# Attention tokens held as 64 rows of 7 chunks, with q and k on alternating partitions

## The chip, the cores and the metric

The kernel runs on one core of a Trainium2 chip. The metric is the device time of one execution in microseconds, as the median of several runs. Beside those runs there is one execution that was recorded by the hardware profiler; all durations of single instructions come from it.

## What is computed

Attention with normalised queries and keys over 8 batches of 12 heads, 448 tokens and 64 features, followed by a token mixer of rank 32 and a two-layer MLP over 768 features with 3072 hidden units:

```python
q_n, k_n = rmsnorm(q, g_q), rmsnorm(k, g_k)             # over the 64 features
attn = softmax(q_n @ k_n.T / 8)                         # 448 x 448, for 96 heads
x = heads_beside_each_other(attn @ v)                   # 8 x 448 x 768
u = x + (x.transpose(0, 2, 1) @ U @ V).transpose(0, 2, 1)   # U 448 x 32, V 32 x 448
out = u + relu(u @ w_ch1) @ w_ch2                       # w_ch1 768 x 3072, w_ch2 3072 x 768
```

## The kernel before

**Layout.** Two neighbouring heads form a pair `p` (48 pairs, 6 to a batch); two pairs form a load group `t` (24 groups). The 448 tokens of a head lie as 112 partitions of 4 tokens each: token 4p + j is row p of chunk j. So q, k and v of a head are loaded as 112 rows of 1024 B (`heads`, `load`, `load_v`; 128 rows are read where there is something behind, and 16 of them are not used). The products are worked on in the chunk order: column c of the queries is row c % 112 of chunk c // 112, and the results for 128 such columns at a time are one tile of x (`OFFS` gives the start of each of the four; odd batches are shifted by 64 columns, so that a tile can hold the end of one batch and the start of the next).

**One pair.** `squares` squares q and k (on GpSimd, a few on ScalarE), `reduce` sums over the features on VectorE into `rs_bank`, `rsqrt` takes the power of -1/2 on ScalarE as Ln and Exp, `scale` multiplies on VectorE and casts to bf16 (`qkn`). The normalised rows are turned so that the features lie on the partitions. Pairs 0 to 11 turn on TensorE (`turn`: 8 transposes into one PSUM bank), and `take_q` and `take_k` copy the result to `qkT`, the first with the gain `gg` = g_q * g_k; pairs 12 to 47 turn by a transposing DMA (`dma_transposes`), and `gains` multiplies on ScalarE in place. Then `scores` makes for each of the 4 chunks of keys a 112 x 448 block for each of the two heads (8 matmuls; their stationary operand is 128 columns of `qkT`, of which 16 belong to what lies behind the chunk, except for pair 0, which takes 112), `expo` takes the exponential of both heads' blocks in one ScalarE instruction (4 to a pair), `products` multiplies E with the values and a column of ones (16 matmuls for each head), and `normalize` divides by the sum (3 VectorE instructions for each head). `cast_v` makes the bf16 values of a group on GpSimd.

**The mixer and the MLP.** `mix_to` forms U's product (`Ub` holds U's rows in the order of the x tiles), `mix_x` and `mix_u` add V's product to x. `mlp` runs 24 groups of 6 matmuls into `hT` (`ph`, then a Relu on ScalarE or VectorE), and then 24 matmuls for each half tile of the output (`po`), adds x and stores the rows by chunks (`store`).

**U.** U comes in the same 112-row layout (`Uf`, `Us`). `setup_U` moves its rows on TensorE with shifted identities (14 matmuls, the word `pU` of the head), and one ScalarE copy (`Ub:a`) brings them to `Ub`. The cast of V's columns into chunk order and two copies to `Vsh` are in `setup_late` (the word `late`), on GpSimd.

**Order.** The scheduler is off (`tc.manual_schedule()`): each engine runs its instructions in the order in which the program issues them. The first batch's attention is written out as the list `HEAD`: `sq` squares, `R` reduce, `q` rsqrt, `S` scale (`Sq` on VectorE and `Sk` on GpSimd for pair 0), `T` transposes (the digit behind a colon is the PSUM bank, a letter the engine: `a` ScalarE, `v` VectorE, `p` GpSimd), `Eq` and `Ek` the copies of q and k, `SC` one chunk's scores, `X` its exponential, `V` the products and `N` the normalisation of one head, `MT`, `t`, `MU`, `u` the mixer of the first batch, `B` the first MLP matmuls that were put ahead, `F` matmuls without use that keep TensorE busy, `w` the loads of weights (GpSimd's queue), `cast` the values' cast, `ld` the loads of U and V, `G` the gain column. After a word named in `ISSUE`, further loads are issued on SyncE's queue. From there on `weave` spreads the next batch's `attention` and `mixing` over the matmuls of the running batch's `mlp`; at the end of the head `mlp(0)` begins with its fifth group.

## Time and profile before

| | |
|---|---|
| median of 5 runs | 600.79 us (600.41 to 603.1) |
| the profiled execution | 602.41 us, of which 600.5 us are the span of its instructions |
| TensorE matmuls busy | 582.7 us, 97% of the span |
| weight loads of TensorE (beside the matmuls) | 319.1 us |
| VectorE, ScalarE, GpSimd busy | 296.1, 264.7, 127.3 us |
| transfers | 72.27 MB, mean 120 GB/s |
| granted TensorE clock, mean | 0.994 |

In the views below, a group of instructions is named by its line, its engine and output<-input. A timeline row gives the start in us, the duration, the instruction, and in brackets how long its engine stood idle ahead of it and which instruction or transfer ended that. A row by stretches gives for each engine its busy us and its instructions, then the granted clock, the share of the DMA engines and GB/s.

### The profile page before, as it was taken

To read this page: it belongs to the slowest core of one execution; us is meant where nothing else is said; L and a number is where in the kernel's file an instruction comes from. 1 tells how busy PE (TensorE), PEld (TensorE's weight loads), DVE (VectorE), ACT (ScalarE), POOL (GpSimd) and SP (SyncE) were. 2 spreads that over 40 slices of the span, in tenths; PEclk is the share of its full clock that TensorE was granted. 3 is DMA by queue.
4 is the path that set the end of the run, shared out by engine and by line. 5 is a ranking of instruction groups with operands and counts; after the bars stand their busy time and mean duration, and the time that the engine had idled before them with its cause. 6 is when DMAs were issued, how large, how long until landed. Compare 5 with 4: busy or idle time off the path is not lost.

```text
span 600.5 us, 11297 instructions
## 1 busy us (share of the span) xinstructions
PE 582.7 (97%) x4723; PEld 319.1 (53%) x4723; DVE 296.1 (49%) x604; ACT 264.7 (44%) x425; POOL 127.3 (21%) x113
## 2 busy tenths in 40 slices
PE   6799998999999999999999999999999999999996
PEld 3465555444565555544565556544465555554563
DVE  4785878345453566454453665545454462521111
ACT  5867551466503772076620875056640476112200
POOL 6793230333030330220330131303303000000000
PEclk9889999999999999999999999999999999999999
DMA  8999995854353544544264652833544210140011
GB/s 269 271 232 238 237 238 82 213 136 121 63 151 83 138 137 126 127 135 70 87 171 67 154 136 51 201 83 97 136 121 106 63 28 6 45 89 0 1 53 52
DMA packets 107799, 72.27 MB, mean 120 GB/s; under 512 B 56616, under 2 KB 104104, under 8 KB 107748
## 3 DMA queue, kind: packets, MB, share of 16 engines
q1 hardware_dynamic: 96292, 61.56, 40.5%
q0 software_dynamic: 11168, 9.73, 9.9%
q8 instruction: 37, 0.61, 0.4%
q10 hardware_dynamic: 288, 0.26, 0.1%
q14 instruction: 14, 0.11, 0.1%
HBM read 56.78 MB, written 11.01 MB: 113 GB/s over the span
## 4 chain that ended last, share of the span: by engine, by line
PE 82%; DVE 2%; ACT 1%; issue 0%; DVEq 0%; ACTq 0%
PE po L406 35%; PE ph L386 33%; PE o L289 6%; PE sc L276 6%; PE px L356 1%; DVE rs_bank L212 1%; PE pm L331 1%; DVE osb L410 1%; ACT E L281 0%; DVE qkn L229 0%; PE px L353 0%; ACT hT L389 0%; PE px L354 0%; DVE x L301 0%; DVE xs L304 0%
## 5 line engine op out<-in xcount | busy, mean ns | idle before, releaser
L281 ACT ACTIVATE E<-sc 112x896 bf16<-112x896 f32 x192 | 172.9, 914 | 176.9 <-PE sc L276 176.8
L406 PE MATMUL po<-w2b,hT 128*128 128x384 bf16 x1344 | 237.7, 326 | 2.2 <-DVE osb L410 1.3
L406 PEld LDWEIGHTS <-hT 128*128 128x128 bf16 x1344 | 126.4, 98 | 90.5 <-issue 11.5
L386 PEld LDWEIGHTS <-w1b 128*128 128x128 bf16 x1128 | 102.7, 98 | 105.6 <-issue 19.7
L209 POOL TENSOR_TENSOR sq<-qk 112x1024 f32<-112x1024 f32 x42 | 79.3, 1896 | 316.3 <-DMA qk<-in_k_dram 247.6
L386 PE MATMUL ph<-uB,w1b 128*128 128x512 bf16 x576 | 132.6, 379 | 0.0
L389 ACT ACTIVATE hT<-ph 128x512 bf16<-128x512 f32 (+1 forms) x122 | 66.8, 547 | 107.1 <-PE ph L386 106.6
L386 PE MATMUL ph<-uA,w1b 128*128 128x384 bf16 x552 | 100.5, 326 | 0.4 <-DVE x L358 0.3
L391 DVE TENSOR_SCALAR hT<-ph 128x384 bf16<-128x384 f32 (+1 forms) x66 | 41.1, 622 | 93.4 <-PE ph L386 93.2
L289 PEld LDWEIGHTS <-E 112*128 112x128 bf16 x1536 | 61.8, 99 | 19.2 <-issue 5.0
L410 DVE TENSOR_TENSOR osb<-po,x 128x384 f32<-128x384 f32 x48 | 26.8, 558 | 73.5 <-PE po L406 73.2
L212 DVE TENSOR_REDUCE rs_bank<-sq 112x16 f32<-112x1024 f32 (+1 forms) x45 | 54.0, 1199 | 8.8 <-ACT sq L207 6.2
L289 PE MATMUL o<-va,E 112*128 112x65 bf16 x1344 | 56.9, 194 | 0.5 <-DVE xs L304 0.5
L276 PE MATMUL sc<-qkT 64*128 64x448 bf16 x376 | 55.2, 359 | 1.4 <-ACT E L281 0.8
L229 DVE TENSOR_TENSOR qkn<-qk,rs_bank 112x1024 bf16<-112x1024 f32 (+1 forms) x46 | 55.2, 1202 | 2.6 <-ACT rs_bank L221 2.4
L300 DVE RECIPROCAL rec<-o 128x4 f32<-128x4 f32 x84 | 15.2, 181 | 70.5 <-PE o L289 70.2
L276 PEld LDWEIGHTS <-qkT 64*128 64x128 bf16 (+1 forms) x384 | 13.4, 95 | 34.8 <-issue 29.4
L358 DVE TENSOR_TENSOR x<-px,x 128x384 bf16<-128x384 f32 x48 | 25.9, 553 | 11.9 <-PE px L356 11.9
L301 DVE TENSOR_TENSOR x<-o,rec 128x192 bf16<-128x192 f32 x84 | 30.0, 357 | 2.9
L195 POOL CAST va<-vt 112x1024 bf16<-112x1024 f32 x23 | 23.9, 1042 | 1.3 <-PE sc L276 1.3
L267 ACT ACTIVATE qkT<-qkT,gg 128x448 bf16<-128x448 bf16 x36 | 23.8, 662 | 0.0
L304 DVE TENSOR_TENSOR xs<-o,rec 64x64 bf16<-64x64 f32 x84 | 18.3, 218 | 0.7
(83 smaller groups left out, 183.2 us busy)
## 6 DMA issues: line engine op xcount, KB each, us to landing
qk<-in_q_dram SPq DMA_DIRECT2D x44, 256.0 KB, 4.7
qk<-in_k_dram SPq DMA_DIRECT2D x44, 256.0 KB, 5.0
vt<-in_v_dram SPq DMA_DIRECT2D x22, 512.0 KB, 5.7
w1b<-in_moe_w_ch_dram POOLq DMA_DIRECT2D x6, 768.0 KB, 18.1
w2b<-in_moe_w_ch_dram POOLq DMA_DIRECT2D x6, 768.0 KB, 38.5
out_dram<-osb SPq DMA_DIRECT2D x8, 336.0 KB, 2.8
out_dram<-osb SPq DMA_DIRECT2D x8, 288.0 KB, 2.9
out_dram<-osb SPq DMA_DIRECT2D x8, 240.0 KB, 2.8
```

The lines of the kernel that those rows point to most:

```text
L209: nc.gpsimd.tensor_tensor(dst, src, src, OP.mult)
L212: nc.vector.tensor_reduce(rs_of(p).rearrange("p (s h j) -> p s h j", s=2, h=2)[:, :, hs], sqs[p].rearrange("p (s h j d) -> p s h j d", s=2 ...
L229: eng.tensor_tensor(qkns[p][:, :, c].rearrange("p j g d -> p g j d"), qk_of[t][0:SP, a].rearrange("p s h (j d) -> p (s h) j d", d=D)[:, c] ...
L276: nc.tensor.matmul(sc[0:n, hh, 0:S], flat[pp, c:c + n], blocks(p)[pp, :, 0], start=True, stop=True)
L281: nc.scalar.activation(Es[p % NE][:, :, PAD + kc * S:PAD + (kc + 1) * S], scs.pop((p, kc))[0:SP, :, 0:S], AF.Exp, scale=float(D) ** 0.5)
L289: nc.tensor.matmul(o[:, i, :], E[:, hh, c:c + P], va[:, hl, kc, :], start=(kc == 0), stop=(kc == NJ - 1))
L301: nc.vector.tensor_tensor(x3[:, :, d0:d0 + D], o[:, t0:t0 + 3, 0:D], rec[:, t0:t0 + 3].rearrange("p c -> p c ()").to_broadcast([P, 3, D]), ...
L386: nc.tensor.matmul(ph, w1b[:, dc, hc * P:(hc + 1) * P], u[:, dc, :], start=(dc == 0), stop=(dc == KD - 1))
L389: nc.scalar.activation(hT[:, hc, 0:n], ph, AF.Relu)
L391: nc.vector.tensor_relu(hT[:, hc, 0:n], ph)
L406: nc.tensor.matmul(po, hT[:, hc, i * P:(i + 1) * P], w2b[:, half, hc], start=(hc == 0), stop=(hc == KH - 1))
L410: nc.vector.tensor_add(osb[:, hs], po, xt[i][:, hs])
```

## The change

Tokens lie as 64 rows of 7 chunks: token 7p + c is row p of chunk c. q's rows go to the even and k's rows to the odd partitions of one 128-partition tile (`qk_of[t][s::2]`), so each squares, reduce and transpose handles q and k together; `load` issues 2 transfers to a group in place of 4, `load_v` 3 in place of 1. `scale` is two instructions, for chunks 0 to 3 and 4 to 6, that write to alternating places of `qkn`, so that the chunk order becomes 0, 4, 1, 5, 2, 6, 3 and two chunks make 128 columns. A pair is turned in 7 transposes of 128 x 128. In the result every second column is a query and every second a key: `take_q` and `gains` read every second column into a tile of their own (`qT`), `take_k` copies the others to the odd columns of `qkT`, and `scores` reads its 128 stationary columns from every second column of `qkT`. The 448 keys are three blocks of 128 and one of 64; the last block's other 64 rows are zero in k, get an exponent of -30000 (`none`), and meet values of chunk 3 loaded a second time. U is loaded twice, to both halves of the partitions, and GpSimd casts it in 4 pieces to `Ub`; V's cast is 3 pieces. `setup_U` and the words `pU` and `Ub:a` are gone. The list `HEAD` is written anew; in place of `Sq`, `Sk`, `Tq`, `Tk` pair 0 has `Se` (chunks 0 to 3, VectorE), `So` (chunks 4 to 6, GpSimd) and one `T`.

```diff
-    NJ = 4
-    SP = S // NJ
+    NC = 7
+    SP = S // NC
...
-    SQK = 2 * NJ * SP
+    NK = 4
...
+    CHUNKS = (0, 4, 1, 5, 2, 6, 3)
...
-    Uf = consts.tile([SP, NJ * rank], FP32, name="Uf")
-    Us = consts.tile([SP, NJ, rank], BF16, name="Us")
+    Uf = consts.tile([P, NC, rank], FP32, name="Uf")
...
-    Es = [consts.tile([SP, 2, PAD + NJ * S + PAD], BF16, name=f"E{i}") for i in range(NE)]
+    Es = [consts.tile([P, 2, PAD + NK * S + PAD], BF16, name=f"E{i}") for i in range(NE)]
-    qkTs = [consts.tile([P, SQK + 16], BF16, name=f"qkT{i}") for i in range(NQ)]
-    qkL = [consts.tile([P, 2, 2, 2, NJ * D], FP32, name=f"qk{i}") for i in range(2)]
-    vL = [consts.tile([P, HG, NJ * D], FP32, name=f"vt{i}") for i in range(2)]
+    qTs = [consts.tile([P, S], BF16, name=f"qT{i}") for i in range(NQ)]
+    qkTs = [consts.tile([P, 2 * NK * P], BF16, name=f"qkT{i}") for i in range(NQ)]
+    qkL = [consts.tile([P, 2, 2, NC * D], FP32, name=f"qk{i}") for i in range(2)]
+    vL = [consts.tile([P, HG, NK * D], FP32, name=f"vt{i}") for i in range(2)]
...
+        nc.gpsimd.memset(none[0:SP], 0.0)
+        nc.gpsimd.memset(none[SP:], -30000.0)
...
     def setup_late():
-        nc.gpsimd.tensor_copy(Us, Uf.rearrange("p (j r) -> p j r", j=NJ))
-        nc.gpsimd.tensor_copy(V4.rearrange("r (j p) -> r j p", j=NJ), Vf.rearrange("r (p j) -> r j p", j=NJ))
+        for par in range(2):
+            for half in range(2):
+                i0, n, c0 = ((0, 4, 0), (0, 3, 4), (1, 3, 4), (0, 4, 0))[2 * par + half]
+                rows = slice(half * SP, (half + 1) * SP)
+                nc.gpsimd.tensor_copy(Ub[rows, par, i0:i0 + n], Uf[rows, c0:c0 + n])
+        Vc = Vf.rearrange("r (p c) -> r c p", c=NC)
+        for half in range(2):
+            at = V4[:, 0:S - SP].rearrange("r (i n p) -> r n i p", n=2, p=SP)[:, half]
+            nc.gpsimd.tensor_copy(at, Vc[:, 4 * half:4 * half + 3])
+        nc.gpsimd.tensor_copy(V4[:, S - SP:], Vc[:, 3])
...
         if part == "U":
-            nc.gpsimd.dma_start(Uf, moe_U.rearrange("(p j) r -> p (j r)", j=NJ))
+            nc.gpsimd.dma_start(Uf.rearrange("p c r -> p (c r)"),
+                                bass.AP(moe_U.tensor, moe_U.offset, [[0, 2], [NC * rank, SP], [1, NC * rank]]))
...
-    def setup_U(pU):
...
     def heads(x, h, n):
-        rows = P if h + n < B * H else SP
-        src = x.rearrange("b h s d -> (b h) s d")[h:h + n].rearrange("h (p j) d -> p h (j d)", j=NJ)
-        (ps, _), (hs, _), (ls, ln) = src.ap
-        return rows, bass.AP(src.tensor, src.offset, [[ps, rows], [hs, n], [ls, ln]])
+        return x.rearrange("b h s d -> (b h) s d")[h:h + n].rearrange("h (p c) d -> p h (c d)", c=NC)
     def load_pair(eng, t, s, a, hs=slice(0, 2)):
-        rows, src = heads((q, k)[s], HG * t + 2 * a + hs.start, hs.stop - hs.start)
-        eng.dma_start(qk_of[t][0:rows, a, s, hs], src)
+        h = HG * t + 2 * a
+        eng.dma_start(qk_of[t][s::2, a, hs], heads((q, k)[s], h + hs.start, hs.stop - hs.start))
     def load(t):
-        for a in range(2):
-            for s in range(2):
-                load_pair(nc.sync, t, s, a)
+        for s in range(2):
+            nc.sync.dma_start(qk_of[t][s::2].rearrange("p a h c -> p (a h) c"),
+                              heads((q, k)[s], HG * t, HG))
     def load_v(t):
-        rows, src = heads(v, HG * t, HG)
-        nc.sync.dma_start(v_of[t][0:rows], src)
+        src = heads(v, HG * t, HG)
+        for rows, c0, c1, at in ((0, 0, 4, 0), (SP, 4, 7, 0), (SP, 3, 4, 3)):
+            nc.sync.dma_start(v_of[t][rows:rows + SP, :, at * D:(at + c1 - c0) * D], src[:, :, c0 * D:c1 * D])
...
-            nc.scalar.activation(copy, rs[:, 8:16], AF.Exp, scale=-0.5)
+            nc.scalar.activation(copy, rs, AF.Exp, scale=-0.5)
...
-    def scale(p, eng=nc.vector, c=slice(0, 4), rs=None):
+    def scale(p, parts=(0, 1), eng=nc.vector, rs=None):
         t, a = divmod(p, 2)
         if p not in qkns:
-            qkns[p] = norm.tile([SP, NJ, 4, D], BF16, tag="qkn", name="qkn", bufs=3)
-        n = c.stop - c.start
-        rs = rs_of(p)[:, c.start * NJ:c.stop * NJ] if rs is None else rs
-        eng.tensor_tensor(
-            qkns[p][:, :, c].rearrange("p j g d -> p g j d"),
-            qk_of[t][0:SP, a].rearrange("p s h (j d) -> p (s h) j d", d=D)[:, c],
-            rs.rearrange("p (g j) -> p g j ()", j=NJ).to_broadcast([SP, n, NJ, D]),
-            OP.mult)
...
-    def turn(p, s, pt):
-        for j in range(NJ):
-            nc.tensor.transpose(pt[:, s, j], qkns[p][:, j, 2 * s:2 * s + 2].rearrange("p h d -> p (h d)"),
-                                ident[:SP, :SP])
+            qkns[p] = norm.tile([P, NC, 2, D], BF16, tag="qkn", name="qkn", bufs=3)
+        rs = (rs_of(p) if rs is None else rs).rearrange("p (h c) -> p h c ()", h=2)
+        for part in parts:
+            c = slice(0, 4) if part == 0 else slice(4, NC)
+            n = c.stop - c.start
+            eng.tensor_tensor(
+                qkns[p][:, part::2].rearrange("p c h d -> p h c d"),
+                qk_of[t][:, a].rearrange("p h (c d) -> p h c d", d=D)[:, :, c],
+                rs[:, :, c].to_broadcast([P, 2, n, D]),
+                OP.mult)
+    def turn(p, pt):
+        for c in range(NC):
+            nc.tensor.transpose(pt[:, c], qkns[p][:, c].rearrange("p h d -> p (h d)"), ident)
+        del qkns[p]
     def take_q(p, pt):
-        nc.vector.tensor_scalar(blocks(p)[:, :, 0], pt[:, 0], gg, None, OP.mult)
+        nc.vector.tensor_scalar(qTs[p % NQ], pt.rearrange("p c r -> p (c r)")[:, 0::2], gg, None, OP.mult)
     def take_k(p, pt, copy=nc.vector.tensor_copy):
-        copy(k_side(p)[:, 0:SQK].rearrange("p (j s r) -> p j s r", j=NJ, s=2)[:, :, 1], pt[:, 1])
+        copy(qkTs[p % NQ][:, 1:2 * S:2], pt.rearrange("p c r -> p (c r)")[:, 1::2])
...
     def dma_transposes(p):
-        nc.sync.dma_start_transpose(out=qkTs[p % NQ][:, 0:SQK].rearrange("p (m r) -> p m r", r=SP),
-                                    in_=qkns.pop(p).rearrange("p j g d -> p (j g d)"))
+        nc.sync.dma_start_transpose(out=qkTs[p % NQ][:, 0:2 * S].rearrange("p (c r) -> p c r", r=P),
+                                    in_=qkns.pop(p).rearrange("p c h d -> p (c h d)"))
     def gains(p):
-        qT = blocks(p)[:, :, 0]
-        nc.scalar.activation(qT, qT, AF.Copy, scale=gg)
+        nc.scalar.activation(qTs[p % NQ], qkTs[p % NQ][:, 0:2 * S:2], AF.Copy, scale=gg)
     def scores(p, kcs):
-        flat, n = k_side(p), SP if p == 0 else P
         for kc in kcs:
             sc = ps_s.tile([P, 2, 512], FP32, tag="s", name="sc")
-            c = (2 * kc + 1) * SP
             for hh in range(2):
                 pp = slice(hh * D, (hh + 1) * D)
-                nc.tensor.matmul(sc[0:n, hh, 0:S], flat[pp, c:c + n], blocks(p)[pp, :, 0],
+                nc.tensor.matmul(sc[:, hh, 0:S], qkTs[p % NQ][pp, 2 * kc * P + 1:2 * (kc + 1) * P:2], qTs[p % NQ][pp],
                                  start=True, stop=True)
             scs[p, kc] = sc
     def expo(p, kc):
-        nc.scalar.activation(Es[p % NE][:, :, PAD + kc * S:PAD + (kc + 1) * S], scs.pop((p, kc))[0:SP, :, 0:S],
-                             AF.Exp, scale=float(D) ** 0.5)
+        nc.scalar.activation(Es[p % NE][:, :, PAD + kc * S:PAD + (kc + 1) * S], scs.pop((p, kc))[:, :, 0:S],
+                             AF.Exp, scale=float(D) ** 0.5, **({"bias": none} if kc == NK - 1 else {}))
...
     def store(b, c0, c1, osb, r0):
-        orow = out[b].rearrange("(p j) d -> j p d", j=NJ)
-        for j, p0, p1, r in segments(c0, c1):
-            nc.sync.dma_start(orow[j, p0:p1, :], osb[r0 + r:r0 + r + p1 - p0, :])
+        orow = out[b].rearrange("(p c) d -> c p d", c=NC)
+        for n in range((c1 - c0) // SP):
+            r = r0 + n * SP
+            nc.sync.dma_start(orow[CHUNKS[c0 // SP + n]], osb[r:r + SP, :])
...
     HEAD = """
-        sq00:a R00 sq01:a R01 q0 gg Sk0 sq1:a G Sq0 Tq0:0 Tk0:1 F8:2 R1 ld:U ld:V sq2:a Eq0 q1 sq3:p
-        Ek0:a S1 SC00 X00 SC01 R2 T1:0 cast0 X01 Eq1 SC02 F1:1 q2 SC03 F3:1 Ek1:v X02 S2 SC10 T2:0
-        sq4:p X03 SC11 X10 R3 Eq2 V00:1 q3 SC12 Ek2:v X11 w10 S3 V01:0 SC13 late X12 R4 T3:2 X13
-        SC20 Eq3 SC21 Ek3:a V11:2 sq5:p X20 N00 V10:1 N01 N10 q4 X21 SC22 S4 pU:0 w11 X22 SC23
-        SC30 Ub:a MT0:0 w12 R5 X23 t0:a T4:1 cast1 SC31 Eq4 X30 V20:0 N11 w13 q5 w14 SC32 Ek4:a S5
-        V21:2 cast2 X31 MT1:1 t1:v SC33 X32 N21 T5:1 Ek5:v X33 SC40 w15 Eq5 MU1:2 w20 SC41 u1:v
-        X40 V31:1 X41 N20 w21 SC42 V30:2 N31 X42 sq6:p SC43 N30 X43 MU0:0 SC50 u0:v MT3:1 t3:v
-        MT2:2 SC51 sq7:p X50 V40:0 R6 X51 SC52 X52 V41:1 N40 SC53 R7 B00 t2:a X53 MU2:0 B01 u2:v
-        V50:2 N50 q6 B10 V51:0 N41 B02 MU3:2 N51 u3:a B11 MT4:1 t4:v B12 MT5:0 S7 MU4:1 t5:a B03
-        MU5:0 u4:a S6 B13 B04 u5:a B14 B05 B15
+        sq00:a R00 sq01:a R01 q0 gg So0 sq1:a G Se0 R1 T0:0 F4:1 Ek0:a ld:U q1 ld:V Eq0 S1 SC00
+        sq2:a sq3:p X00 SC01 F1:0 R2 X01 T1:0 cast0 q2 SC02 F1:1 Ek1:v X02 Eq1 SC03 F3:0 S2
+        sq4:p SC10 X03 T2:0 R3 X10 Eq2 SC11 F1:1 SC12 w10 q3 Ek2:v X11 R4 late V00:1 V01:0 X12
+        S3 SC13 SC20 X13 N01 T3:2 q4 SC21 Eq3 X20 V11:0 X21 sq5:p Ek3:v SC22 S4 V10:2 N11 w11
+        X22 N10 SC23 X23 SC30 w12 T4:0 X30 R5 cast1 MT1:2 SC31 X31 t1:v SC32 V21:2 Eq4 q5 w13
+        Ek4:v SC33 N00 MT0:0 w14 X32 V20:1 S5 t0:a SC40 X33 cast2 N20 T5:0 Eq5 SC41 X40 w15
+        V31:1 SC42 w20 Ek5:v X41 N21 MU1:0 N31 w21 X42 MT2:2 SC43 X43 u1:v V30:1 sq6:p N30 SC50
+        t2:a MU0:0 X50 SC51 u0:v X51 V41:1 N41 SC52 sq7:p MT3:0 X52 V40:2 R6 t3:a SC53 X53 MU2:1
+        u2:a MU3:0 N40 B00 u3:a V50:2 R7 B01 N50 MT4:0 t4:a V51:1 N51 q6 B02 B10 B03 B11 S7
+        MT5:0 t5:a MU4:1 u4:v B12 MU5:0 u5:v B13 B04 B14 S6 B05 B15
     """
```

## The prediction

> **What bounds the kernel now.** I read the page's busy shares first.
>
> ```profile
> PE 582.7 (97%) x4723; PEld 319.1 (53%) x4723; DVE 296.1 (49%) x604; ACT 264.7 (44%) x425; POOL 127.3 (21%) x113
> ```
>
> TensorE holds the kernel on average, but the change touches mostly the other engines. So I asked for the stretches: the start, the head's two halves with the slow part between them, the first MLP, and the rest.
>
> ```profile
> 0.00:12.50 12.50, 8.19 (x35) 3.44 (x37) 4.92 (x7) 6.06 (x12) 7.68 (x29) 1.00 0.81 257
> 12.50:25.70 13.20, 10.85 (x146) 6.67 (x145) 11.26 (x21) 12.07 (x22) 9.05 (x10) 1.00 1.12 284
> 25.70:34.20 8.50, 6.48 (x74) 4.12 (x72) 5.22 (x16) 5.59 (x9) 8.50 (x10) 0.60 1.18 252
> 34.20:45.75 11.55, 11.27 (x156) 7.30 (x153) 9.98 (x27) 7.69 (x15) 9.76 (x8) 1.00 1.21 229
> 45.75:105.00 59.25, 56.83 (x541) 32.78 (x539) 44.91 (x92) 28.58 (x47) 15.18 (x10) 1.00 1.04 198
> 105.00:600.50 495.50, 489.09 (x3783) 264.78 (x3780) 219.81 (x444) 204.71 (x323) 77.13 (x49) 1.00 0.40 98
> ```
>
> From 105 us on TensorE is busy for 489.1 of 495.5 us, 4.6 of the rest being the end. There only fewer or shorter TensorE instructions help. Before 45.75 us the head is a chain over all engines. Its worst stretch is 25.70 to 34.20, where GpSimd is busy all the time and the granted clock is 0.60. GpSimd's timeline says why.
>
> ```profile
> 8.56 0.70 POOL L609 TENSOR_TENSOR grow<-grow 1x64 f32<-1x64 f32 x2 [3.95 <-DMA grow<-in_g_k_dram]
> 9.22 1.03 POOL L229 TENSOR_TENSOR qkn<-qk,rk 112x512 bf16<-112x512 f32 x1
> 10.21 0.75 POOL L147 DMA_DIRECT2D Uf<-in_moe_U_dram  x1
> 10.95 0.73 POOL L149 DMA_DIRECT2D Vf<-in_moe_V_dram  x1
> ...
> 21.65 1.00 POOL L131 CAST V<-Vf 128x448 bf16<-128x448 f32 x1 [4.09 <-DMA Vf<-in_moe_V_dram]
> ...
> 23.10 1.89 POOL L209 TENSOR_TENSOR w2b<-hT 112x1024 f32<-112x1024 f32 x1
> 24.95 1.72 POOL L166 DMA_DIRECT2D w1b<-in_moe_w_ch_dram  x2
> 26.64 1.06 POOL L195 CAST va<-vt 112x1024 bf16<-112x1024 f32 x1
> ```
>
> The gains land at 8.56, hence the late scale of pair 0 and the late issue of U and V; V lands at 21.65, and behind its cast stand a square, two weight issues and the values' cast of group 1. TensorE stands before that cast:
>
> ```profile
> 27.76 1.04 PE L289 MATMUL bank<-va,E 112*128 112x65 bf16 x16 [2.02 <-POOL va L195]
> ```
>
> After this gap 16 products take 1.04 us instead of 0.68, until about 34.2.
>
> **The change part by part.**
>
> *Start.* Ahead of the gains in the queues stand 1024 KB of q and k (four transfers of 128 KB, two of 256), landed by 7.96 (issue at 2.16 plus 5.8 to landing); now 896 KB. An eighth of some 6 us is 0.75; I take 0.7, ends 0 and 1.0. GpSimd's scale of pair 0 has 384 elements: from its rows on GpSimd, 1.03 us for 512 and 1.89 for a square of 1024, 0.82 us, so 0.2 less. So U's load starts 0.85 us sooner, at about 9.35. The seven transposes end at about 9.85. Pair 0's copy of k no longer stands behind `q1`, which held it to 11.10; behind it now stands a square of 0.95 us (0.63 for 512 elements, 1.06 for 1024). First exponential: 9.85 + 0.55 + 0.95 = 11.35, now 12.78. This 1.4 us reaches the end only as far as the next wait moves too.
>
> *U and V on GpSimd.* V: 10.1 + its 10.7 us to landing = 20.8. U landed in 6.3 us when read once; now it is read twice by one transfer, as V is read four times. Ends: 6.3, and 13.4, the longest of the q and k loads then; I take 10.7, as V's is the only repeated load: 20.05. Four casts at 0.30 (the row of Us) end at 21.25. V's 448 elements in three pieces cost 1.00 plus two starts, 1.25 in all, the two copies 0.45: 22.95 against 23.10. The square shrinks by an eighth to 1.66; with 1.72 and 1.0 the values' cast ends at 27.3, against 27.7: gain 0.4. With U at 6.3 us it is 0.85; with 13.4 it is a loss of 2.3. [...]
>
> *What stands behind that cast.* Today the waiting products (`V20`) are queued ahead of `SC32`, so ScalarE runs dry after `X31`. The new list has `SC32` ahead of `V21`: one exponential more (0.85 us) is done in the gap. Gain 0.85. The gap itself stays about 2 to 2.5 us, so the slow clock may come again. If it does, the stretch behind it holds as much TensorE work as before and gives some 0.2 back: 0.4 + 0.85 - 0.2, 1.05 us in all. If it does not, the four gaps of ScalarE before its exponentials from 28 to 33.65 us (1.27, 0.79, 0.46, 0.32) shrink to that of the wait: some 1.8 more, 2.85. The trace has one such gap, and the clock slowed after it; how near it was to not slowing no row tells, so I take the middle, 1.95.
>
> *No TensorE for U.* 14 matmuls (0.5 us) and a ScalarE copy (0.39) leave, at 23 us, ahead of the gap: they lengthen it by what they save. Nothing.
>
> *VectorE.* Reduces have 896 elements for 1024: 1.22 becomes 1.09 (from 0.70 for 512). The two scales, 0.69 (the row for 512) and 0.56, less overlap, against 1.21: nothing. The copies from PSUM read every second bf16 column: today 0.45 and 0.38; upper end the f32 cast of 384 elements, 0.558, plus 64 more, 0.63 and 0.69. So per pair of the first twelve -0.13 to +0.35 us; I take +0.35, the row that reads a 4-byte step. In the head the wait above hides it. From 45.75 to 85 us VectorE is busy three quarters of the time: +0.1. From 85.8 to 96.8 the chain that ended last runs over VectorE with three reduces and two scales and no copies: -0.4, of which TensorE, which waits there 1.7 us in four pieces, gets half. Together -0.1.
>
> *Scores.* Same 384 matmuls, same 448 columns, same 192 exponentials of 896. New is the stationary operand with a step of two columns, of which the trace has no example. The nearest rows are contiguous:
>
> ```profile
> L276 PEld LDWEIGHTS <-qkT 64*128 64x128 bf16 x376 | 12.8, 94 | 33.8 <-issue 28.4 <-ACT rs_bank L221 1.6 <-ACT E L281 1.3
> ...
> L276 PEld LDWEIGHTS <-qkT 64*112 64x112 bf16 x8 | 0.7, 124 | 1.1 <-issue 0.9
> ```
>
> The load of 112 columns takes longer than that of 128. Bounds: 0, and these 30 ns for each load if a step costs the same; no gain, as the number of columns stays. I take 0, since the operand has 128 columns as the faster row. [...]
>
> *At nothing.* DMA transposes: 36 of 112 x 1024 become 128 x 896, the same bytes, 1.22 us each on SyncE, two pairs ahead; uncovered, 36 times any excess, on a queue that idles most of the time. `load_v` adds two issues of 0.4 us to a group, `load` drops two of 0.45. `gains` (0.66) on ScalarE, under half busy after 105 us. Stores keep two transfers to a tile. The weights land ahead of their use by 5 us at least (issue at 36.5 plus 39.0, used at 80.6), so 2 us less head still fits, the more with fewer bytes of q and k.
>
> *Sum:* -1.95 - 0.1, about -2.0 us. The profiled execution's 602.41 (span 600.5 and 1.9 around it) would become 600.4; it stood 1.6 above the median, so I apply the difference to the median 600.79: 598.8, from 599.6 (slow clock again) to 597.9 (not). A measurement here tells 0.3% from no change, 1.8 us.
>
> **The rivals.**
>
> *A, slower: the stepped weight load.* Outside the head stand 336 of the 384 loads, on the engine without slack. Pair 0's four matmuls with loads of 112 took 0.58 us, those with 128 columns 0.55: 7.5 ns each, 2.5 us in all; with the full 30 ns, 10.1. That gives 601.3 to 608.9, say 605. It decides from 6 ns a load (2.0 / 336) and is slower by 0.3% from 11. For it: both loads of a chunk stand ahead of two matmuls that run side by side, and two of these pairs take 0.49 us where 448 columns each go through. Against it: the unchanged number of columns.
>
> *B, U lands late.* At 13.4 us to landing the cast loses 2.3, the exponential ahead of it gives 0.85: 2.3 - 0.85 + 0.2 - 0.1 = +1.55 with the slow clock, -0.25 without: 602.3 to 600.5, say 601.5. For it: U lands first in GpSimd's order, so V's cast stands behind it. Against it: V's row.
>
> *C, the gap closes.* If V lands 2 us sooner, because the queues hold fewer and longer pieces, TensorE does not wait and the clock stays: a further 2.0 us on the lower end, 595.9. Against it: U's casts alone would hold GpSimd until 21.25.
>
> **How the numbers follow.** The forecast has 0.62, of which 0.38 beyond 1.8 us and 0.24 within; A 0.20 (0.18 slower, 0.02 within); B 0.10 (0.07 within, 0.03 slower); C 0.08 (faster). So faster 0.46, same 0.33, slower 0.21. The range 596.4 to 606.0 leaves out C and the upper two fifths of A, 0.16 together; the forecast's own is 597.5 to 600.2.
>
> **What would show it.** The first exponential at about 11.4 us; U landing by 20; the values' cast ending at 27.3; `mlp(0)` starting about 43.8 instead of 45.75; the stretch after it as long as now. Weight loads of the scores above 100 ns, or pairs of their matmuls longer than 0.36 us after 105 us, would prove A. U's casts starting after 21.5 would prove B. A copy from PSUM near 0.4 us would void VectorE's surplus.

## The result: 604.60 us against 601.09, slower by 0.5%

The changed kernel took 604.60 us in the median of 24 runs (600.95 to 607.36), the kernel before 601.09 us beside it (45 runs, 599.76 to 604.96). The ratio is 1.0054 (1.0041 to 1.0067). On a second chip it was 1.0030 (1.0006 to 1.0054). The prediction said 598.8; its range reached up to 606.0 for rival A, which is not what happened. That 604.60 lies inside that range is luck: the forecast was a gain, and the part of the range above 602.3 was there for a cost that did not arise.

The profiled execution of the changed kernel took 603.29 us (span 601.5). It lies 1.3 below its median, while that of the kernel before (602.41) lies 1.3 above its own. So the two profiles show 1.0 us (in their spans) of a loss of 3.5; the rest of it has to be looked for in what varies between executions.

The stretches of the changed kernel, as the prediction showed them for the kernel before: busy us and instructions of PE, PEld, DVE, ACT, POOL, then granted clock, share of the DMA engines, GB/s.

```profile
0.00:12.50 12.50, 9.02 (x42) 3.85 (x42) 5.88 (x9) 6.95 (x14) 9.28 (x32) 1.00 0.78 218
12.50:25.70 13.20, 8.07 (x85) 4.54 (x83) 8.86 (x16) 8.53 (x15) 7.27 (x13) 0.80 1.13 219
25.70:34.20 8.50, 7.67 (x108) 4.88 (x107) 8.14 (x25) 7.55 (x12) 8.50 (x10) 0.90 1.17 263
34.20:45.75 11.55, 11.40 (x154) 7.48 (x153) 10.03 (x29) 7.35 (x15) 8.91 (x8) 1.00 1.20 225
45.75:105.00 59.25, 55.74 (x527) 31.91 (x526) 45.60 (x97) 28.90 (x47) 15.19 (x12) 1.00 1.06 200
105.00:600.50 495.50, 490.16 (x3789) 265.38 (x3787) 214.00 (x480) 207.70 (x323) 69.83 (x49) 1.00 0.41 95
```

Two rows tell of a loss. From 12.5 to 25.7 us TensorE is busy for 8.07 us (10.85 before), the slow clock has moved here, and the DMA engines move 219 GB/s in place of 284 at the same busy share. From 45.75 to 105 us TensorE idles 1.1 us more. GpSimd's timeline shows what stands first:

```profile
6.52 0.70 POOL L582 TENSOR_TENSOR grow<-grow 1x64 f32<-1x64 f32 x2 [1.13 <-DMA grow<-in_g_k_dram]
7.96 1.01 POOL L149 DMA_DIRECT2D Uf<-in_moe_U_dram  x1
8.96 0.72 POOL L152 DMA_DIRECT2D Vf<-in_moe_V_dram  x1
...
19.18 1.68 POOL L200 TENSOR_TENSOR w2b<-hT 128x896 f32<-128x896 f32 x1 [5.03 <-DMA hT<-in_k_dram]
...
26.36 1.74 POOL L159 DMA_DIRECT2D w1b<-in_moe_w_ch_dram  x2
28.08 1.06 POOL L185 CAST va<-vt 128x1024 bf16<-128x1024 f32 x1
```

The gains land early, as forecast. Then the square of pair 4 (`sq4`; the expectations call it the fourth pair's) waits 5.0 us for the keys of group 2 (`load(2)`): issued at 8.36 us, landed at 19.2. Before the change pair 4's keys were there in time, and the square ran without a wait:

```profile
14.54 1.89 POOL L209 TENSOR_TENSOR w2b<-hT 112x1024 f32<-112x1024 f32 x1
```

All of GpSimd's list stands behind it, and TensorE's wait there is the longest of the head:

```profile
22.77 0.29 PE L231 MATMUL bank<-ident,qkn 128*128 128x128 bf16 x1 [4.31 <-DVE qkn L223]
```

What TensorE waits for here is the scale of pair 3 (`S3`), which needs nothing from these keys. It is late because the new `HEAD` has the reduce of pair 4 (`R4`) ahead of it on VectorE, and `R4` waits for the square. In the list before the change `S3` stood first. VectorE in the changed kernel, then before:

```profile
20.89 1.10 DVE L203 TENSOR_REDUCE rs_bank<-w2b 128x14 f32<-128x896 f32 x1 [3.86 <-POOL w2b L200]
22.02 1.15 DVE L223 TENSOR_TENSOR qkn<-qk,rs_bank 128x512 bf16<-128x512 f32 x2
```

```profile
17.99 1.22 DVE L229 TENSOR_TENSOR qkn<-qk,rs_bank 112x1024 bf16<-112x1024 f32 x1
19.31 1.23 DVE L212 TENSOR_REDUCE rs_bank<-w2b 112x16 f32<-112x1024 f32 x1
```

So the late keys reach TensorE at once through this order of two words. No run puts `S3` back ahead of `R4`, so how much of the loss belongs to the new list, and how much to the loads, is open.

To follow the runs I use three marks of each profile: the start of `mlp(0)` (its first products into `ph`), the time from there to the start of the row of 42 `po` products near 105 us, called the middle, and the rest of the span. The rest is 496.2 to 496.8 us in every run of the table, so the whole matter lies in the first two. A profile is one execution, and it can lie well off its kernel's median, which stands beside it.

| profiled execution | its us | its kernel's median | `mlp(0)` starts | middle |
|---|---|---|---|---|
| before | 602.41 | 601.09 | 45.75 | 58.49 |
| changed | 603.29 | 604.60 | 45.53 | 59.77 |
| changed, second profile (y1_after) | 605.28 | 604.46 | 47.09 | 60.20 |
| U in two transfers (x1_u_two) | 600.05 | 603.13 | 42.18 | 59.85 |
| copies of runs (y2_takes) | 602.51 | 602.12 | 46.08 | 58.45 |
| both (y3_u_two_takes) | 601.12 | 601.15 | 43.95 | 59.10 |
| v in one transfer (z1_v_one) | 600.45 | 601.02 | 42.53 | 59.95 |
| v in two (z3_v_two) | 602.24 | 601.50 | 44.59 | 59.62 |
| before, v in three (w4_before_v3) | 604.55 | 606.01 | 43.84 | 62.17 |
| before, v in three, every second row (q1_before_v3_spread) | 604.13 | 603.57 | 44.48 | 61.14 |
| before, v in two (q2_before_v_halves) | 603.93 | 607.67 | 44.27 | 61.40 |

### The profile page after: what moved, and what is told of

Same layout as the page of the kernel before. It is cut to its first block, busy times and chain, and to the rows that moved or that the text cites. A ratio compares the mean times of both kernels' runs of the same rounds, so it can differ in the third digit from the quotient of the medians.

```text
span 601.5 us, 11296 instructions
## 1 busy us (share of the span) xinstructions
PE 582.1 (97%) x4695; PEld 318.0 (53%) x4695; DVE 292.5 (49%) x652; ACT 267.0 (44%) x423; POOL 119.0 (20%) x121
## 4 chain that ended last, share of the span: by engine, by line
PE 82%; DVE 2%; ACT 1%; POOL 0%; issue 0%; ACTq 0%
PE po L390 35%; PE ph L370 33%; PE o L272 6%; PE sc L258 6%; PE px L339 1%; PE pm L314 1%; DVE osb L394 1%; ACT E L264 0%; DVE qkn L223 0%; DVE rs_bank L203 0%; PE px L336 0%; POOL sq L200 0%; ACT hT L373 0%; DVE x L284 0%; PE px L337 0%
## 5 line engine op out<-in xcount | busy, mean ns | idle before, releaser
L264 ACT ACTIVATE E<-sc 128x896 bf16<-128x896 f32 x144 | 130.1, 915 | 173.2 <-PE sc L258 173.2
L200 POOL TENSOR_TENSOR sq<-qk 128x896 f32<-128x896 f32 x42 | 69.8, 1683 | 323.6 <-DMA qk<-in_k_dram 304.4
L272 PEld LDWEIGHTS <-E 128*128 128x128 bf16 x1536 | 61.4, 99 | 17.1 <-issue 2.2
L258 PE MATMUL sc<-qT,qkT 64*128 64x448 bf16 x384 | 56.5, 359 | 2.9 <-ACT E L264 1.1
L272 PE MATMUL o<-va,E 128*128 128x65 bf16 x1344 | 56.6, 194 | 1.0 <-DVE xs L287 0.8
L223 DVE TENSOR_TENSOR qkn<-qk,rs_bank 128x384 bf16<-128x384 f32 (+1 forms) x91 | 52.2, 615 | 2.9 <-ACT rs_bank L212 2.7
L203 DVE TENSOR_REDUCE rs_bank<-sq 128x14 f32<-128x896 f32 (+1 forms) x45 | 48.1, 1069 | 7.7 <-ACT sq L198 4.9
L264 ACT ACTIVATE E<-sc,none 128x896 bf16<-128x896 f32 x48 | 48.2, 1003 | 0.7 <-PE sc L258 0.6
L185 POOL CAST va<-vt 128x1024 bf16<-128x1024 f32 x23 | 23.9, 1042 | 3.6 <-DMA vt<-in_v_dram 3.6
L251 ACT ACTIVATE qT<-qkT,gg 128x448 bf16<-128x448 bf16 x36 | 23.8, 662 | 0.0
```

Source lines behind the costliest of these rows:

```text
L200: nc.gpsimd.tensor_tensor(dst, src, src, OP.mult)
L203: nc.vector.tensor_reduce(rs_of(p).rearrange("p (h c) -> p h c", h=2)[:, hs], sqs[p].rearrange("p (h c d) -> p h c d", h=2, d=D)[:, hs], A ...
L223: eng.tensor_tensor(qkns[p][:, part::2].rearrange("p c h d -> p h c d"), qk_of[t][:, a].rearrange("p h (c d) -> p h c d", d=D)[:, :, c], r ...
L258: nc.tensor.matmul(sc[:, hh, 0:S], qkTs[p % NQ][pp, 2 * kc * P + 1:2 * (kc + 1) * P:2], qTs[p % NQ][pp], start=True, stop=True)
L264: nc.scalar.activation(Es[p % NE][:, :, PAD + kc * S:PAD + (kc + 1) * S], scs.pop((p, kc))[:, :, 0:S], AF.Exp, scale=float(D) ** 0.5, **({ ...
L272: nc.tensor.matmul(o[:, i, :], E[:, hh, c:c + P], va[:, hl, kc, :], start=(kc == 0), stop=(kc == NK - 1))
```

## The experiments

Each ratio is to the kernel before on the same chip. The x runs, the z runs and the w runs each had a chip of their own; y and q shared another. The changed kernel itself was measured in the first measurement (1.0054) and beside the y runs (1.0030), and what a variant gains is set against these two; a difference of some 0.3% between two ratios is not clear of their intervals. Packet times are means over the trace's packets of one size in SyncE's queue.

**U, the grain of q and k, and V.** The first theory: U's load is led by a repeat of two, sits on few engines, and holds the spread loads there. Of this the changed kernel's trace shows that 24 packets of U, of 4480 bytes, run from 12.3 to 16.3 us in two rows side by side, and that two of its sixteen completions come at 17.35 and 17.77 us, the other fourteen by 15.48. Its rivals: the transfers of four heads are too large, or the 64-row ones slow as such.

x1_u_two:

```diff
-  nc.gpsimd.dma_start(Uf..., bass.AP(moe_U.tensor, moe_U.offset, [[0, 2], [NC * rank, SP], [1, NC * rank]]))
+  for half in range(2):
+      nc.gpsimd.dma_start(Uf[half * SP:(half + 1) * SP]..., moe_U.rearrange("(p c) r -> p (c r)", c=NC))
```

> The changed kernel, but U is loaded by two transfers of 64 rows (one for each half of the partitions) instead of one transfer that is led by a repeat of two. Theory 1 (U's transfer lies on 2 of the 16 engines and holds up there every load that is spread over all): U lands in about 6 us instead of 9.8, the keys of group 2 land by about 16.5 us instead of 19.2, GpSimd's wait of 5.0 us ahead of the fourth pair's square falls to 2.5 or less, and the time is 2 to 3 us below the changed kernel. Theory 2 (one transfer for four heads makes pair 4 wait for pair 5's rows too) and theory 3 (transfers of 64 rows are slower as such): the wait stays above 4 us and the time within 1 us of the changed kernel.

603.13 us, ratio 1.0006 (0.9982 to 1.0029). The wait is halved, and no more:

```profile
16.00 1.68 POOL L201 TENSOR_TENSOR w2b<-hT 128x896 f32<-128x896 f32 x1 [2.53 <-DMA hT<-in_k_dram]
```

This profile is the fastest of that kernel's executions, but the second chip agrees on the wait: 5.25 us in y2_takes, 2.92 with U in two (y3_u_two_takes). U is a part of the wait; the other 2.5 us must have another cause. The ratio alone does not show a gain: its interval overlaps that of the changed kernel on the second chip (1.0006 to 1.0054).

x2_pair_loads issues four transfers to a group (`for a in range(2): for s in range(2): load_pair(nc.sync, t, s, a)`).

> The changed kernel, but each group's q and k come in four transfers of two heads, in the order first pair's q and k, second pair's q and k, as before the change. Theory 2 (size of the transfers): half of the group's 896 KB need not have landed for pair 4, some 2 us at 220 GB/s, so the wait of 5.0 us falls to about 3 and the time by 1 to 2 us. Theory 1 (U's two engines): the queue of those two engines is the same, only its order changes; the wait falls by at most 1 us. Theory 3 (64 rows slower as such): as theory 2.

603.41 us, 1.0003 (0.9989 to 1.0018). The engines moved still less, 200 GB/s from 12.5 to 25.7 us. The wait only changed its place: the values' cast of group 0 waited 4.05 us for v, and the square began at 19.64 us (19.18 in the changed kernel). A finer grain of q and k did not bring it sooner.

x3_uv_spread has U in two and V in four plain transfers, V's on ScalarE's queue (`nc.scalar.dma_start(Vf[i * rank:(i + 1) * rank], moe_V)`); x4_before_v4 gives V's alone to the kernel before.

> The changed kernel, but U is loaded by two transfers of 64 rows, and V by four transfers of 32 rows on ScalarE's queue instead of one transfer led by a repeat of four on GpSimd's. Theory 1: no engine holds more than another, so beyond the two-part U alone the last engines' delay of some 2 to 3 us in the loads of 15 to 25 us goes as well; the keys of group 2 land by 16, the wait ahead of the fourth pair's square is below 2 us, and the time is 3 to 5 us below the changed kernel, below the kernel before. Theories 2 and 3: within 1 us of the changed kernel.

> The kernel before the change, but V is loaded by four transfers of 32 rows on ScalarE's queue instead of one transfer led by a repeat of four on GpSimd's queue. Theory 1: V lands well under the 10.7 us of before, GpSimd's wait of 4.1 us ahead of V's cast shrinks to 2 or less, TensorE's gap of 2.0 us at 26 to 28 us closes, and the time is 1 to 3 us below the kernel before. If repeats do not matter (theories 2 and 3), V lands in about 10 us as now and the time stays within 0.7 us.

602.54 us, 0.9991 (0.9972 to 1.0011), and 604.75 us, 1.0031 (1.0018 to 1.0045). Neither decides: V's four issues hold ScalarE itself, from 9.57 us for 2.7 us in the first and from 9.72 for 5.8 us in the second, so that the first exponential comes at 13.17 and 18.08 us. In the first the square still began at 19.61, behind other waits; in the second ScalarE ran nothing for 7.3 us, the issues included. The first has one of the lowest ratios although in its profile (603.84, 1.3 above its median) the square began no sooner; that is a warning that the start of this square alone may not set the time.

**VectorE's copies, and the order.** y1_after is the changed kernel itself. y2_takes transposes against a permuted identity, so that q and k of a chunk come out as two runs of 64 columns; pairs 0 to 11 then have contiguous keys too:

```diff
-  nc.tensor.transpose(pt[:, c], ..., ident)
+  nc.tensor.transpose(pt[:, c], ..., sorter)
-  nc.vector.tensor_scalar(qTs[p % NQ], pt.rearrange("p c r -> p (c r)")[:, 0::2], gg, None, OP.mult)
+  nc.vector.tensor_scalar(qTs[p % NQ].rearrange("p (c r) -> p c r", r=SP), pt[:, :, 0:SP], gg, None, OP.mult)
-  copy(qkTs[p % NQ][:, 1:2 * S:2], pt.rearrange("p c r -> p (c r)")[:, 1::2])
+  copy(qkTs[p % NQ][:, S:2 * S].rearrange("p (c r) -> p c r", r=SP), pt[:, :, SP:])
```

y3_u_two_takes adds U's two transfers, y4_u_two_takes_order also puts `load(2)` ahead of `load_v(0)`.

> The changed kernel itself, for its ratio on the chip of the other three. If its loss belongs to the kernel (U's load of one transfer holds the fourth pair's keys by 5 us, and VectorE's copies cost about 1 us later): 1.005 of the kernel before, as in the first measurement (1.0041 to 1.0067), with the fourth pair's square starting near 19 us. If it belonged to that one chip: 1.000.

> The transposes go against a sorted identity, so that q and k leave PSUM as runs of 64 columns instead of every second column; the first twelve pairs' k lies contiguous, the score operand too. Nothing else. Theory V (the copies from PSUM cost TensorE about 1 us from 45 to 105 us): the copies fall from 0.68 and 0.65 us to about 0.45 and 0.38, TensorE's idle time from 45.75 to 105 us falls by about 1 us, time 0.5 to 1.5 us under the changed kernel. Rival (the loss is the head's alone): the copies get shorter and TensorE's idle time stays, time the same within 0.3 us. Both: the square of the fourth pair still waits some 5 us for its keys. Score weight loads stay at 95 ns.

> The same with U loaded by two transfers of 64 rows in place of one that repeats. Theory U (the repeat-led transfer of U holds back the keys of the third group): 3 to 4 us under the changed kernel with the clock at 1.00 from 25.7 to 34.2 us, that is 0.994 to 1.000 of the kernel before; the fourth pair's square waits 2.5 us as in the run with U in two transfers alone. Rival (the loads of 64 rows are slower as such): no more than 1 us under the changed kernel, the wait back at 4 to 5 us.

> The same with the third group's q and k issued ahead of the first group's v on SyncE. If the issue order is what is left of the wait: the fourth pair's square waits 1 us or less, the first values' cast starts about 1.3 us later and is waited for, 1 to 2 us under the run before it, about 0.995 of the kernel before. If the queues' rate is: the wait passes to the values' cast, time the same as the run before it within 0.6 us.

| run | us | ratio |
|---|---|---|
| y1_after | 604.46 | 1.0030 (1.0006 to 1.0054) |
| y2_takes | 602.12 | 0.9998 (0.9978 to 1.0019) |
| y3_u_two_takes | 601.15 | 0.9996 (0.9973 to 1.0019) |
| y4_u_two_takes_order | 604.47 | 1.0032 (1.0014 to 1.0050) |

The loss came again on the second chip. The copies are the second part of it. In the changed kernel, by line: durations in ns (least, median, most), first and last start, and shapes.

```profile
L235 DVE TENSOR_SCALAR qT<-pt,gg x6: 682/684/684, 47.1 to 83.5; 128x448 bf16<-128x448 bf16 x6
L238 DVE COPY qkT<-pt x6: 648/649/658, 47.7 to 84.1; 128x448 bf16<-128x448 bf16 x6
```

The same two in y2_takes:

```profile
L239 DVE TENSOR_SCALAR qT<-pt,gg x6: 449/450/452, 47.6 to 82.7; 128x448 bf16<-128x448 bf16 x6
L242 DVE COPY qkT<-pt x6: 379/380/381, 48.0 to 83.0; 128x448 bf16<-128x448 bf16 x6
```

Reading every second column cost 234 and 269 ns a copy. TensorE's waits for them in the changed kernel were these (the second is for `x`, which VectorE writes behind them):

```profile
53.88 1.15 PE L370 MATMUL ph<-uA,w1b 128*128 128x384 bf16 x6 [0.21 <-DVE qkT L238]
71.59 1.14 PE L370 MATMUL ph<-uA,w1b 128*128 128x384 bf16 x6 [0.48 <-DVE x L341]
78.37 0.55 PE L258 MATMUL sc<-qT,qkT 64*128 64x448 bf16 x4 [0.55 <-DVE qkT L238]
84.80 0.69 PE L272 MATMUL o<-va,E 128*128 128x65 bf16 x16 [0.21 <-DVE qkT L238]
```

In y2_takes TensorE has none of these four waits, and the middle is 58.45 us, as before the change (58.49). The ratios agree with a gain but their intervals overlap (0.9978 to 1.0019, 1.0006 to 1.0054). The keys' wait stays (5.25 us). y4_u_two_takes_order refutes the order of issue as the rest: GpSimd then waited 6.66 us for v.

**v's pieces.** What had not been tried was `load_v`: three transfers of 64 neighbouring rows, of 1024, 768 and 256 bytes to a row, in place of one of 128 rows. z1_v_one loads v as before the change: its rows are then not those that the weights of the sums belong to, so it gives wrong sums and is a measurement only, no remedy. z3_v_two drops the third piece (its rows set to zero once), z4_all is y3_u_two_takes with that. z2_halves puts q on rows 0 to 63 and k on rows 64 to 127 for the first six groups:

```diff
-  eng.dma_start(qk_of[t][s::2, a, hs], ...)
+  eng.dma_start(qk_of[t][s * SP:(s + 1) * SP, a, hs], ...)      # t < 6, load() likewise
```

> The changed kernel with v loaded as in the kernel before: one transfer of 128 rows of 1024 bytes for each group, in place of three of 64 rows (1024, 768 and 256 bytes). The rows are then not those that the scores' chunks want, so the weighted sums are left wrong; all instructions on the engines stay. Theory P (v's short 64-row pieces slow everything that runs beside them): the packets of q and k from 12.5 to 25.7 us fall from 130 ns for 1792 bytes to about 100, the fourth pair's square waits under 2 us instead of 5, 2 to 3 us under the changed kernel. Theory U (U's transfer on few engines): packets and wait stay as they are, time within 0.6 us.

> The changed kernel with q on rows 0 to 63 and k on rows 64 to 127 for the first six groups in place of even and odd rows; both leave PSUM as runs of 64 columns, as with the sorted identity. Theory E (a transfer to every second row is slow): packets of 1792 bytes fall towards 100 ns from 12.5 to 25.7 us, the wait under 2 us, 2 to 3 us under the changed kernel beside the 1 to 2 us of the shorter copies. Rival: packets and wait as in the run with the sorted identity, time the same as its 602.1 within 1 us; or worse, if 64 neighbouring rows are slower than 64 spread ones.

> The changed kernel without v's third piece: the 64 KB for each group that only rows of no weight read are set to zero once. Theory P by number of pieces: 256 packets of 30 ns over 16 engines, 0.5 us for each of the three first groups, so the fourth pair's square waits about 4.3 us, and the time falls by 0.5 to 1 us. If pieces do not matter: no difference above 0.3 us.

> U in two transfers, the sorted identity and no third piece of v together. If the costs add: 601.2 less 0.5 to 1 us, 0.996 to 0.999 of the kernel before. If the head is bound by the rate of the queues whatever the pieces: as the run without the third edit, 0.9996.

| run | us | ratio | 1792-byte packet, 12.5 to 25.7 us |
|---|---|---|---|
| changed (first profile) | 604.60 | 1.0054 (1.0041 to 1.0067) | 130 ns |
| z1_v_one | 601.02 | 0.9988 (0.9971 to 1.0006) | 83 ns |
| z2_halves | 605.80 | 1.0064 (1.0042 to 1.0087) | 146 ns |
| z3_v_two | 601.50 | 0.9994 (0.9975 to 1.0013) | 109 ns |
| z4_all | 601.37 | 0.9991 (0.9974 to 1.0008) | 111 ns |

z1_v_one by stretches, the same stretch, and its square of the fourth pair:

```profile
12.50:25.70 13.20, 10.28 (x120) 5.80 (x120) 12.96 (x28) 12.73 (x22) 10.52 (x17) 1.00 1.13 281
```

```profile
15.41 1.68 POOL L201 TENSOR_TENSOR w2b<-hT 128x896 f32<-128x896 f32 x1 [2.00 <-DMA hT<-in_k_dram]
```

The rate is back (281 GB/s for 219), the wait is 2.0 us and the clock is not lowered there (0.80 from 25.7 to 34.2 us), with U's repeat-led load still in place. Not all of that is the rows: with one issue for three, SyncE issued the keys of group 2 at 7.02 us in place of 8.36, so 1.3 of the 3.8 us by which the square began sooner are issue time. z2_halves went the other way: q and k on neighbouring rows made it 191 GB/s, and the copies' gain was lost. Not every transfer of 64 rows is slow: those to every second row were the better ones (130 ns and 219 GB/s in the changed kernel, 146 ns and 191 GB/s in z2_halves). z3_v_two had been expected to cut the wait to 4.3 us and gain 0.5 to 1 us; the wait fell to 2.67 (the keys were issued 0.7 us sooner) and the ratio to 0.9994. Why the third piece, 64 KB of short packets, costs so much in the changed kernel no run shows; there the number and shortness of the pieces remains a rival to the rows they write. z4_all shows that the gains do not add; its keys came earlier, then V came late.

**The suspected cost put into the kernel before.** Only `load_v` is edited there.

```diff
 # w4_before_v3
+ for r0, r1, c0, c1 in ((0, 64, 0, 4), (64, rows, 0, 3), (64, rows, 3, 4)):
+     nc.sync.dma_start(v_of[t][r0:r1, :, c0 * D:c1 * D], src[r0:r1, :, c0 * D:c1 * D])
 # q1_before_v3_spread: the same pieces, of rows s:rows:2 (s = 0, 1, 1)
 # q2_before_v_halves: rows 0 to 63 and 64 on, all 1024 bytes
```

> The kernel before with each group's v in three pieces, of 64 rows by 1024 bytes and 64 rows by 768 and 256, the same data. Theory P: its packets of q and k from 12.5 to 25.7 us rise from 58 ns for 1024 bytes to 70 or more, DMA falls from 284 to about 240 GB/s, and it loses 1 to 3 us: 1.002 to 1.005. Rival (the pieces hurt only beside 64-row loads of q and k): packets under 62 ns, time the same.

> The kernel before with each group's v in three pieces of 64 rows by 1024, 768 and 256 bytes as in the run that lost 0.7%, but of every second row in place of 64 neighbouring ones. If neighbouring rows are the cost: packets of 1024 bytes near 60 ns from 12.5 to 25.7 us (58 before, 78 in that run), 280 GB/s, 1.000 to 1.002 of the kernel before. If short packets and the number of transfers are: as that run, 70 ns or more, 1.004 to 1.010.

> The kernel before with each group's v in two transfers of 64 neighbouring rows, all packets 1024 bytes. If neighbouring rows are the cost: packets 70 ns or more, 230 to 250 GB/s, 1.003 to 1.007. If short packets are: near 60 ns, 1.000 to 1.002.

| v's transfers in the kernel before | 1024-byte packet, 12.5 to 25.7 us | GB/s there | ratio |
|---|---|---|---|
| one, 128 rows | 58 ns | 284 | 1 |
| q1: three, every second row | 62 ns | 234 | 1.0027 (1.0006 to 1.0047) |
| q2: two, 64 neighbouring rows | 76 ns | 235 | 1.0083 (1.0053 to 1.0113) |
| w4: three, 64 neighbouring rows | 78 ns | 222 | 1.0070 (1.0040 to 1.0100) |

The stretch from 12.5 to 25.7 us in w4, then in q1:

```profile
12.50:25.70 13.20, 9.97 (x134) 6.19 (x134) 12.09 (x26) 12.32 (x24) 10.66 (x13) 0.98 1.17 222
```

```profile
12.50:25.70 13.20, 10.22 (x124) 6.08 (x122) 9.91 (x21) 10.36 (x19) 8.54 (x11) 0.83 1.00 234
```

In this kernel neighbouring rows cost the most: q2, with no short packet, lost 0.83% and q1 0.27%, on one chip and with intervals apart. Some 0.27% stays with three pieces to spread rows, against 1.000 to 1.002 expected; w4 and q2 lost more than their forecasts. The cleanest number is v's 768-byte packet between 200 and 400 us, where the DMA engines' share is 0.54 and 0.48: 60.2 ns to 64 neighbouring rows (w4), 37.6 ns to every second row (q1). q1 missed its forecast of the rate: it is lower at a lower busy share (1.00), with packets nearly as quick as before, which points to engines without work for part of the time; its square of the fourth pair still waited 4.59 us. In q1 each load of that group shows twelve of its sixteen completions first and four some 2 to 4 us later (12.4 to 14.0 and 16.3 to 17.4 us for the one that ends as the square starts), and V's load is led by a repeat of four; in the kernel before, at most four of its 40 packets of 5376 bytes run at a time, and four of its sixteen completions come from 19.5 to 21.6 us, the others by 18.0. That V's load sits on the same four engines is argued, not shown.

In w4 the loss does not stand in the head at all: `mlp(0)` starts at 43.84. In q1, where the square waited 4.59 us with `S3` ahead of `R4`, TensorE's longest wait in the head behind it was 2.16 us and `mlp(0)` starts at 44.48. In both the weights come late, and TensorE meets them in the middle (w4, then q1):

```profile
81.54 0.48 PE L407 MATMUL po<-w2b,hT 128*128 128x384 bf16 x2 [1.47 <-DMA w2b<-in_moe_w_ch_dram]
81.14 0.48 PE L407 MATMUL po<-w2b,hT 128*128 128x384 bf16 x2 [2.50 <-DMA w2b<-in_moe_w_ch_dram]
```

In q2 this wait is 2.76 us. So it comes with v in pieces whatever their rows, and what neighbouring rows add in time stands in the medians alone: the profiles of q1 and q2 differ by 0.2 us, their medians by 4.1. Where in the execution that time is lost no kept profile shows.

**An attempt at v's right rows in whole transfers.** w1_v128 loads each head's v in one transfer over 128 rows, the source led by its two halves; w2_v128_sorter and w3_v128_sorter_u2 add the permuted identity and U's two transfers.

```diff
+ for h in range(HG):
+     nc.sync.dma_start(v_of[t][:, h], bass.AP(src.tensor, src.offset + h * hs, [[4 * D, 2], [ls, SP], [1, 4 * D]]))
```

> The changed kernel with v's right rows loaded over all 128 rows at once: four transfers to a group, one for each head, each of 128 rows of 1024 bytes (chunks 0 to 3 to the lower half, 4 to 7 to the upper one, the last of these a row of no weight). Theory P (transfers to 64 neighbouring rows slow all that runs beside them): q's and k's packets of 1792 bytes at 85 to 100 ns from 12.5 to 25.7 us, the fourth pair's square waits about 2 us, 2 to 3 us under the changed kernel, 0.998 to 1.000 of the kernel before. Rival (it was the number of transfers or their issue): 4 issues of 0.6 us for 3, wait and time as in the changed kernel.

> The same with the sorted identity for the first twelve pairs' copies. If the two losses are separate and add: 1 us less, 0.996 to 0.999 of the kernel before, mlp(0)'s first instruction near 42 us and fewer waits for VectorE from 45 to 105 us.

> The same with U in two transfers of 64 rows. By theory P these two transfers, to 64 neighbouring rows each, save nothing more: as the run before it within 0.6 us. If U's repeat-led transfer costs on its own: another 1 to 2 us less, 0.994 to 0.997.

686.05, 687.21 and 687.01 us, 1.14 each: none of the three expectations came. GpSimd in w1_v128:

```profile
24.22 1.04 POOL L190 CAST va<-vt 128x1024 bf16<-128x1024 f32 x1 [12.93 <-DMA vt<-in_v_dram]
```

v's four transfers of 128 KB end with two completions each, at 12.5 and 12.8, 18.0 and 18.1, 21.0 and 21.1, 24.0 and 24.1 us, the last ones 3 us apart, as 64 packets of 49.9 ns in a row take (3.2 us). From 16.5 to 18.0 us the share of the 16 DMA engines stands between 0.1 and 0.2 (two are 0.125), at 47 GB/s. So each ran on two engines, though the leading dimension of two is no repeat. The three runs thus say nothing on whether the remedies add.

No version beat the kernel before by more than its interval.

## Why the prediction was wrong

*The start (U's load 0.85 us sooner, the first exponential 1.4): the size was read from an unusual execution.* The 1.4 us were left out of the sum; the 0.85 went into its 0.4. The first exponential came at 11.28 us, as forecast (11.35). But the 12.78 that it was compared with is not what the kernel before usually does. In w4_before_v3, whose loads up to the gains are those of the kernel before, the gains land and the first exponential starts here (GpSimd, then ScalarE):

```profile
6.26 0.70 POOL L610 TENSOR_TENSOR grow<-grow 1x64 f32<-1x64 f32 x2 [1.66 <-DMA grow<-in_g_k_dram]
```

```profile
11.57 1.72 ACT L282 ACTIVATE E<-sc 112x896 bf16<-112x896 f32 x2 [0.65 <-PE sc L277]
```

In q1 and q2 it is 11.38 and 11.07 us, with the gains used from 5.92 and 6.34. The 8.56 of the profile of before was a late landing, which that execution, 1.6 us above the median of the first five, had and these three had not. U's load was issued at 7.57 to 7.99 us in these three and at 7.96 in the changed kernel, so nothing of the 0.85 is left. The first exponential comes at 10.72 to 12.60 in the two profiles of the changed kernel and in x1, y2 and z1. So the change gained nothing here, and the prediction had the warning in its own sum: it noted the 1.6 us and subtracted a gain that was probably part of them.

*"`load_v` adds two issues of 0.4 us to a group", at nothing: the step that failed.* I priced the issues and the bytes of the three pieces and not where they write. The issues came out as priced: pair 4's keys were issued at 8.36 us, before the change at 8.42. They landed late. The values' cast of group 1 was to end at 27.3 and ended at 29.1; `mlp(0)` was to start at 43.8 and started at 45.53 and 47.09. With v whole it starts at 42.53. The runs give 0.4 to 0.7% to the pieces: the ratio falls from 1.0030 or 1.0054 to 0.9988 without them, and rises to 1.0070 when the kernel before has them. The rows show in the packets: from 12.5 to 25.7 us the 1024-byte packets of SyncE's queue took 78 ns with v to neighbouring rows (w4) and 62 with v to every second row (q1), the 1792-byte ones 146 ns with q and k on neighbouring rows (z2_halves) and 130 on every second row (the changed kernel). What in the hardware makes this difference no run shows.

*U's load: the landing right, the effect on others not priced.* It landed in 9.8 us (10.7 taken), 17.8 in all (by 20). Rival B's sign, casts after 21.5, came (21.71), though not by U: they stood behind the square. What U's load cost was the keys: x1 cut the wait from 5.0 to 2.5 us, and the ratio to 1.0006, by some 0.2 to 0.5%, which is not clear of the intervals; beside the shorter copies it gained nothing (0.9996 in y3, 0.9998 in y2).

*The gap and the slow clock (-1.95).* The sum took the gap at the values' cast, 2 to 2.5 us, with one exponential more in it. The gap moved to 22.8 us and grew to 4.3, ahead of pair 3's transposes, with `R4` ahead of `S3` and `R4` waiting for late keys; the clock fell to 0.80 and 0.90 around it. Neither end of that term applied, and the new order of `S3` and `R4` was not priced.

*VectorE (-0.1): mis-sized.* The upper end taken for the copies was right: 0.68 and 0.65 us, 1.33 together, against 0.63 and 0.69, 1.32. Reduces fell to 1.09 as computed. What was wrong is "VectorE is busy three quarters of the time: +0.1": TensorE's next operands stand directly behind the copies. The middle grew by 1.28 us. y2_takes gives all of it back; y3_u_two_takes, at 59.10, only half, as a wait for `xs` grew there to 1.97 us (1.30 in y2, 0.78 in the changed kernel). z4_all, with the same copies, has 60.10, with that wait at 2.27 and the clock at 0.97. Why that wait differs is not shown, so that the copies cost 1.3 us rests on y2.

*Rival A is refuted.* The scores' weight loads with a step of two columns:

```profile
L258 PEld LDWEIGHTS <-qkT 64*128 64x128 bf16 x384 | 13.3, 95 | 36.2 <-issue 32.6 <-DVE qkT L238 0.9 <-DMA qkT<-qkn 0.4
```

95 ns against 94, and their matmuls a median of 360 ns: the sum's 0 was right. Two pairs of them take 0.55 us in both kernels, not the prediction's 0.49.

*Put together:* with 1.3 of the 3.5 us in the middle, the head lost about 2.2, where -1.95 had been forecast. The 2.2 is what is left over, not a reading: the only profile of the kernel before has the late gains in its head. What v's pieces (0.4 to 0.7%), U's load (0.2 to 0.5%) and the copies (1.3 us) cost one by one comes to more than the whole, and z4_all shows that mending several gives little more than mending one: each seems to hide behind the next landing. How the head's loss divides among them, and how much of it the order of `S3` and `R4` carries, stays open.

## What to carry to other kernels

Price a transfer also by the rows it writes and by what leads its pattern: transfers to 64 neighbouring rows slowed the packets beside them (58 to 76 ns in q2), one led by a dimension of two ended with two completions and took 3 us for 128 KB (w1), and the wait came up at an instruction that had nothing to do with it. Before moving words in a list, ask what each will stand behind when a load is late. Before counting a wait's removal as gain, see how far the profiled execution lies above its median, and whether that wait is what put it there. Copies that grow right ahead of TensorE's operands cost it time even where their engine idles a quarter of the stretch: here 1.3 us of the 3.0 by which those of six pairs grew.

## What was not expected of the hardware

The exponential with a per-row bias took longer than the one without, on the same shape: 1003 ns (48 instructions) against 915 (144). It costs nothing here, as ScalarE is under half busy (44% of the span). A 1024-byte packet of v took 62 to 66 ns to 64 neighbouring rows in quiet queues (the changed kernel and its variants, 200 to 400 us), 48 to 53 where whole transfers write 112 or 128 rows (z1_v_one, and the kernel before, there with q's and k's packets).
